# Four edits in the prologue of a Fourier mixing and tanh-shrink kernel: an earlier load, two moves on another queue, a load on two queues, another warm-up

## The chip, the cores and the metric

The kernel runs on one core of a Trainium2 chip. The metric is the device time of one execution in microseconds (us); the runs of one kernel are compared by their median. A core has a matrix engine (TensorE, PE in the profile; its weight loads are PEld), three engines for elementwise work (VectorE or DVE, ScalarE or ACT, GpSimd or POOL) and a sync engine (SP) that only issues transfers. Transfers (DMAs) are issued from the queues of SP, ACT and POOL and are carried out by 16 DMA engines that all queues share. Each engine works through its instructions in program order. Matrix products land in PSUM, which PE writes and DVE and ACT read; everything else on the chip lies in SBUF.

## The reference

The input is 8 batches of 3008 tokens with 256 channels. Per batch, the token axis is Fourier transformed, multiplied with a complex filter and transformed back; then every token goes through a small network with g = h - tanh(h):

```
X = np.fft.rfft(x, axis=1)
Y = X * (filt_r + 1j * filt_i)[None, :, :]
y = np.fft.irfft(Y, n=x.shape[1], axis=1).astype(np.float32)
h = y.reshape(8 * 3008, 256) @ w_in          # 256 x 2048, float64 in
g = h - np.tanh(h)
out = (g @ w_out).astype(np.float32)         # 2048 x 256, float64 in
```

## The kernel before, in words

The length 3008 is split as 64 x 47, so the transform is two steps of small matrix products with a twiddle in between. After the first step the data of one batch is 4 blocks of 32 frequencies by 24 rows. `SLOTS` cuts the 32 frequencies into 7 groups: six of 5 (120 partitions) and a leftover one, group 6, of 2. The leftover group is folded: its 48 rows hold the left half of the channels and 48 more partitions the right half, so it works on 96 partitions with 128 columns. Two transfers inside SBUF do that folding, one for its data and one for its filter; both are the function `under` (L943).

The program has a prologue, for batch 0, and then a long pipeline over groups of tokens (`groups`, 4 units of work each, counted by `U`). From the second token group on, PE has next to no pause; later batches' transforms are worked in between the token products. `first`, `middle` and `last` are generators of that pipeline; `last(0)` (`pu`, L447, copied by ACT to `ut`, L450) begins it, and `up_plain` (L555) follows.

The prologue, in program order:

- Three DMAs' worth of half matrices (`fh`) and x of batch 0 in three chunks `c` of 8 rows (`xs`), each chunk in two halves; the right part of a half comes by POOL's queue. VectorE makes the matrices `f0` from `fh` (L1018, L1021). `filt` is three buffers for filters; the first column block of `filt[2]` is set to 1 and serves as operand of the warm-up.
- `tiled()` (L903): matmuls on these ones whose results nobody reads.
- `first0(c)` (L888): first step for batch 0, 32 PE instructions a chunk (a matmul here is two instructions); the copies (L891) go to ACT, two of the last chunk's to VectorE, into `turnt`.
- Loads of weights. `converted` turns float64 weights into float32 sums by bit work: one load of 512 KB (`raw`, L151), one ACT instruction (L157), six of VectorE (L159 to L177). `jobs[0:5]` are worked in the prologue, the others later; `convert(n)` makes n steps of it.
- `across(g)` (L933, L937): PE transposes group g of `turnt` into a tile `a2`; `forth` (L301): products `pa`, `pb`; `filtered` (L306 to L330): seven to nine instructions, mainly VectorE's, with one of POOL (L327) for groups 0 to 4; `back0` (L970, L972) and, for group 6, `back` (L349): products `pe`, copied by ACT (L975, L352) and written to DRAM as `ct2` (POOL's queue for groups 0 to 4, ACT's for 5, ACT's and SP's for 6).
- The loop over g from 0 to 6 runs these staggered: filters and `across` for g+2, `forth` for g+1, `filtered` for g, `back0` for g-1. `filters_of(g)` (L950, L953) issues six loads (nine for group 6) on POOL for groups 0 and 1 and on SP for the others. A buffer is used again after three groups, so the loads for group g wait for `filtered(g-3)`.
- At g = 3, behind the filters of group 5, SP also issues the matrix `gt` of the first token group (L427, 256 KB) and x of batch 1's first 8 rows (`load_x`, L231, L234, L237, 1 MB in a buffer that an x chunk of batch 0 held).
- After the loop `rest` (L960) reads `ct2` of batch 0 back, turned, as `e2` for the first token group: once for the 25 frequencies of groups 0 to 4, and after `way_back()` of the leftover group for the last 7. Each call is four loads, for four blocks, on SP.
- Behind it, in program order: the first loads of batch 2 (`first`), `convert(100)`, the next weight conversion, `first1` (x of batch 1's first rows through the first step, L1059, L1063, L1064), four steps of weight conversion, and `warmer(10)` (L898), 20 PE instructions whose result nobody reads. Then `pu`.

`under` in the kernel before:

```
def under(t):
    nc.sync.dma_start(t[KL:KH, :, 0:DM // 2], t[0:KL, :, DM // 2:DM])
```

It is called in `across(6)`, which is reached at g = 4, and for the filter at g = 5, ahead of `convert(3)` and `way_back()`.

Of the kernel before, what the change touches and what calls it, by code (L numbers as in the profile page):

```python
# [17 lines left out]
BATCH, SEQ, DM = 8, 3008, 256  # L18
NQ, NR = 64, 47
NA = NQ // 2  # L20
NH = (NR + 1) // 2
SG = 5
# [7 lines left out]
KM = SG * NH  # L30
KL = SLOTS[-1][1] * NH
KH = 2 * KL
# [65 lines left out]
def kernel(  # L98
# [9 lines left out]
    nc = tc.nc  # L108
    V, G, ACT = nc.vector, nc.gpsimd, nc.scalar
# [13 lines left out]
    def dram(t, off, dims):  # L123
        return bass.AP(tensor=t, offset=off, ap=[list(d) for d in dims])
# [86 lines left out]
    def begun(tiles, job, queue=nc.sync):  # L211
        j = converted(tiles, *job, queue)
        next(j)
        return j
# [14 lines left out]
    def load_x(t, b, r, n):  # L229

        nc.sync.dma_start(t[0:64, 0:n, :], dram(x.tensor, (b * SEQ + r) * DM,  # L231
                                                [[NR * DM, 64], [1, n * DM]]))
        if r == 0:
            nc.sync.dma_start(t[64:128, 0, :], dram(x.tensor, b * SEQ * DM,  # L234
                                                    [[NR * DM, 64], [1, DM]]))
        lo = 1 if r == 0 else 0
        nc.sync.dma_start(t[64:128, lo:n, :], dram(x.tensor, (b * SEQ + NR - r - lo) * DM,  # L237
                                                   [[NR * DM, 64], [-DM, n - lo], [1, DM]]))
        return t
# [182 lines left out]
    def load_e2(b, c, parts=None, tiles=None):  # L422

        e2, gt = tiles or (tr.tile([128, CH, DM], F32, tag="e2", bufs=2, name="e2"),
                           tr.tile([128, CH, 128], F32, tag="gt", bufs=2, name="gt"))
        if tiles is None:
            nc.sync.dma_start(gt, g_d[:, CH * 128 * c:CH * 128 * (c + 1)])  # L427
        if parts is None:
            nc.sync.dma_start(e2, dram(ct2[b], CH * c * DM, [[NH * DM, 128], [1, CH * DM]]))
        return e2, gt  # L430
# [422 lines left out]
    with tc.tile_pool(name="tr", bufs=2) as tr, tc.manual_schedule():  # L853
# [12 lines left out]
        with tc.tile_pool(name="pro", bufs=1) as pro, \  # L866
                tc.tile_pool(name="ps0", bufs=6, space=bass.MemoryType.PSUM) as ps0:

            def z0(name, shape):
                return ps0.tile(shape, F32, tag="z", bufs=6, name=name)  # L870
# [3 lines left out]
            def big(shape, dtype, name):  # L874

                return pro.tile(shape, dtype, tag="big", bufs=3, name=name)
# [23 lines left out]
            def tiled():  # L900

                t = filt[2][:, 0]
                banks = [z0("warm", [128, 256]) for _ in range(4)]  # L903

                def mm(rows, cols, bank):
                    nc.tensor.matmul(bank[cols], t[rows, 0:cols.stop - cols.start],
                                     t[rows], start=True, stop=True)

                half = slice(0, 64), slice(64, KM)
                out = slice(0, 64), slice(64, 128)  # L910
                for _ in range(6):
                    mm(slice(0, KM), slice(0, 128), banks[0])
                for n in range(4):
                    for i, rows in enumerate(half):
                        for cols in out:
                            mm(rows, cols, banks[2 * (n % 2) + i])
                for n in range(4):
                    for i, rows in enumerate(half):
                        mm(rows, slice(0, 128), banks[2 * (n % 2) + i])
                for _ in range(2):  # L920
                    mm(slice(0, KM), slice(0, 128), banks[0])

            def across(g):

                a, s = SLOTS[g]
                n = s * NH
                t = tr.tile([KM, 4, DM], F32, tag="a2", bufs=2, name="a2")
                for v in (1, 0):
                    pq = z0("pq", [128, 2, DM])
                    for k in range(2):  # L930
                        at = (2 * v + k) * NA + a
                        for h in range(2):
                            nc.tensor.transpose(  # L933
                                pq[0:n, k, h * 128:h * 128 + 128],
                                turnt[:, h, at:at + s].rearrange("p a r -> p (a r)"), one)
                    copy = ACT.copy if g or v else V.tensor_copy
                    copy(t[0:n, 2 * v:2 * v + 2], pq[0:n])  # L937
                if g == len(SLOTS) - 1:
                    under(t)
                return t  # L940

            def under(t):
                nc.sync.dma_start(t[KL:KH, :, 0:DM // 2], t[0:KL, :, DM // 2:DM])  # L943

            def filters_of(g):

                t, queue = filt[g % 3], G if g < 2 else nc.sync
                if g == len(SLOTS) - 1:
                    V.memset(t[0:1, 2:4], 0.0)
                    queue.dma_start(t[NH:KL, 2:4], dram(filt_d, (turned * 4 + 2) * DM,  # L950
                                                        [[4 * DM, NH], [1, 2 * DM]]))
                for v, row, n, src in filter_rows(g):
                    queue.dma_start(t[row:row + n, v], src)  # L953
                return t

            def rest(a, n, queues):

                e2 = e2s[0][0]
                for j in range(4):
                    queues[j % len(queues)].dma_start(  # L960
                        e2[NA * j + a:NA * j + a + n],
                        dram(ct2[0], (NA * j + a) * NH * DM, [[NH * DM, n], [1, CH * DM]]))
# [39 lines left out]
            for c in range(3):  # L1002
# [16 lines left out]
                for to, cols in ((64, slice(0, 64)), (95, slice(63, 64)), (127, slice(31, 32))):  # L1019
                    n = cols.stop - cols.start  # L1020
# [26 lines left out]
            def convert(n):  # L1047

                for _ in range(n):
                    next(early, None)  # L1050
# [3 lines left out]
            def first1(x1):  # L1054

                for r in range(0, 8, 2):
                    pf = z0("pf", [128, 2, DM])
                    for k in range(2):
                        nc.tensor.matmul(pf[:, k], f0[:, r + k], x1[:, r + k],  # L1059
                                         start=True, stop=True)  # L1060
                    a1 = (pro.tile([128, 2, DM], F32, tag="e1", bufs=5, name="a1") if r < 4 else
                          tr.tile([128, 2, DM], F32, tag="a1", bufs=2, name="a1"))
                    ACT.copy(a1, pf)  # L1063
                    (ACT if r < 4 else nc.sync).dma_start(  # L1064
                        dram(ct1[1], r * DM, [[NH * DM, 128], [1, 2 * DM]]), a1)
                    yield
# [3 lines left out]
            last_g = len(SLOTS) - 1  # L1070
            summed = (last_g,)

            def there0(g):
                there = forth(g, a2.pop(g), z0)
                xy = next(there)
                next(there)
                return there, xy
# [3 lines left out]
            def way_back():  # L1081

                product, what = ended.pop(0)
                for _ in product(*what) or ():
                    pass
# [4 lines left out]
            for g in range(last_g + 1):  # L1090
                if g + 2 <= last_g:
                    fts[g + 2] = filters_of(g + 2)
                    a2[g + 2] = across(g + 2)
                if g == 3:
                    e2s[0] = load_e2(0, 0, ())
                    ones_1 = first1(load_x(big([128, 8, DM], F32, "x1"), 1, 0, 8))
                if g == last_g - 1:
                    under(fts[last_g])
                    convert(3)
                    way_back()  # L1100
                if g < last_g:
                    there[g + 1] = there0(g + 1)
                next(there[g][0])
                if g < last_g - 1:
                    convert(3)
                xy = there.pop(g)[1]
                chain = filtered(g, xy, fts.pop(g), V, V if g >= last_g - 1 else G, pro)
                nn = next(chain)
                for _ in range(2):
                    next(chain)  # L1110
                if g in summed:
                    next(chain)
                ended.append((back, (0, g, xy, z0, (ACT, nc.sync))) if g in summed else (back0, (g, nn)))
                if g not in (0, last_g - 1):
                    way_back()
                if g == 2:
                    ahead = [begun(tiles1, job, queue=G) for job in jobs[5:7]]
            rest(0, SG * (last_g - 1), [nc.sync])
            way_back()
            rest(SG * (last_g - 1), NA - SG * (last_g - 1), [nc.sync])  # L1120
            fs = first(2, z1, [(1, c) for c in range(4, NX)])
            next(fs)
            convert(100)
# [9 lines left out]
        with tc.tile_pool(name="dn", bufs=2) as dn, \  # L1133
# [59 lines left out]
            for U in range(total + 2):  # L1193
                i, u = divmod(U, 4)
# [120 lines left out]
```

## Time and profile before

| what | value |
|---|---|
| runs shown | 2701.81, 2702.39, 2700.45 us; median 2701.81 |
| profiled execution | 2702.15 us, span of its instructions 2700.3 us |
| TensorE clock granted, mean | 0.998 |
| warm-up (L906) | 64 PE instructions, 1.45 to 11.13 us |
| `first0` (L888) | 96 PE instructions, 11.13 to 22.0 us |
| VectorE, 40 to 60 us | 15.9 of 20 us busy |
| first product of the token work (`pu`, L447) | 85.44 us |
| PE idle from 0 to 120 us | 15.8 us |
| PE idle from 160 us to the end | 12.4 of 2540 us |
| moved in the first 110 us | 25.32 MB, mean 230 GB/s |

How to read it: times are from the start of the span. A line of the timeline has the start, the length, engine, line, operation, out<-in, the shape (for PE, rows*columns of the array, then the moving operand), the count, and in brackets the idle time ahead of it and what ended it. An engine with a q is its queue: it waits or issues a transfer. In the list of waits the numbers are the total in us, how often, and the longest. The chain of waits goes back from the last instruction, at each step to what released it. A DMA line in it runs from issue to landing. The granted clock is 1.00 at full speed.

### The profile page before, as it was taken

What the parts mean: (1) busy time and instruction counts of PE and PEld (TensorE: products, weight loads), DVE (VectorE), ACT (ScalarE), POOL (GpSimd) and SP (SyncE); (2) the same over time, 40 slices, a digit from 0 to 9 for tenths busy, and PEclk for the clock granted to TensorE, in tenths of its full rate; (3) what the DMA queues carried; (4) which work ended last, traced back from release to release, by engine and by line L of the source; (5) the groups of instructions that cost most, each with busy time, mean ns of one, the idle gap of its engine ahead of it and who ended that gap; (6) DMA issues with size and microseconds to landing.
All of it is one profiled execution on the core that took longest, in us unless ns stands there. A gap on an engine that the chain in (4) does not pass through costs nothing.

```text
span 2700.3 us, 36549 instructions
## 1 busy us (share of the span) xinstructions
PE 2670.9 (99%) x12950; PEld 2360.7 (87%) x12950; DVE 1651.3 (61%) x2083; ACT 1722.8 (64%) x2595; POOL 1289.9 (48%) x1082
## 2 busy tenths in 40 slices
PE   8999999999999999999999999999999999999998
PEld 7578889988898888988889888898889988898887
DVE  6777766666566664666546665566655666544545
ACT  3566666666666666666666666666666666666665
POOL 4124555454454445545445554455445554554552
PEclk9999999999999999999999999999999999999999
DMA  8754223431242223323233232323322231110110
GB/s 219 233 162 115 56 58 77 107 86 49 63 110 75 80 56 78 98 69 81 54 96 80 68 86 57 92 76 79 88 55 58 52 79 34 31 40 19 24 24 18
DMA packets 341400, 208.09 MB, mean 77 GB/s; under 512 B 227096, under 2 KB 303492, under 8 KB 341144
## 3 DMA queue, kind: packets, MB, share of 16 engines
q1 hardware_dynamic: 298957, 147.45, 22.6%
q10 hardware_dynamic: 38138, 45.63, 5.5%
q0 software_dynamic: 4112, 12.60, 1.7%
q8 instruction: 104, 1.70, 0.3%
q14 instruction: 89, 0.72, 0.1%
HBM read 133.42 MB, written 74.97 MB: 77 GB/s over the span
## 4 chain that ended last, share of the span: by engine, by line
PE 93%; DMA 2%; DVE 2%; ACT 1%; issue 1%; SPq 1%; ACTq 0%; POOL 0%; DVEq 0%
PE o L655 40%; PE x L485 23%; PE z L485 11%; PE y L485 6%; PE pu L447 3%; PE pe L349 3%; PE pf L262 2%; PE pa L301 2%; PE pb L301 1%; PE o L709 1%; DMA gt<-g 0%; DMA mats_sb<-mats 0%; DMA f<-f 0%; ACT y L597 0%; PE o L555 0%
## 5 line engine op out<-in xcount | busy, mean ns | idle before, releaser
L655 PE MATMUL o<-t,wd 128*128 128x256 f32 (+1 forms) x3008 | 759.7, 375 | 0.0
L607 DVE TENSOR_TENSOR h<-h,y 128x1024 f32<-128x1024 f32 (+1 forms) x384 | 513.3, 1337 | 295.7 <-ACT y L603 295.2
L465 POOL TENSOR_TENSOR t<-h 128x512 f32<-128x512 f32 (+1 forms) x186 | 254.1, 1366 | 907.7 <-DVE h L607 836.1
L655 PEld LDWEIGHTS o<-t,wd 128*128 128x128 f32 x3008 | 570.5, 190 | 67.2
L485 PE MATMUL x<-tu,wu 128*128 128x256 f32 (+1 forms) x2256 | 573.0, 376 | 1.6 <-ACT u L491 1.1
L655 PE MATMUL o<-h,wd 128*128 128x256 f32 (+1 forms) x2256 | 570.4, 375 | 1.8 <-DVE h L607 1.8
L485 PEld LDWEIGHTS x<-tu,wu 128*128 128x128 f32 x2256 | 421.5, 190 | 57.5 <-ACT u L491 9.6
L655 PEld LDWEIGHTS o<-h,wd 128*128 128x128 f32 x2256 | 424.2, 190 | 50.3 <-DVE h L607 2.6
L491 ACT COPY s<-x 128x512 f32<-128x512 f32 (+1 forms) x188 | 108.6, 578 | 501.9 <-PE x L485 483.8
L597 ACT ACTIVATE y<-h 128x1024 f32<-128x1024 f32 (+1 forms) x384 | 400.2, 1042 | 13.3 <-ACT a L263 5.2
L600 ACT ACTIVATE y<-y 128x1024 f32<-128x1024 f32 (+1 forms) x384 | 399.2, 1039 | 12.1
L603 ACT ACTIVATE y<-y 128x1024 f32<-128x1024 f32 (+1 forms) x384 | 399.9, 1041 | 7.8 <-DMA x_sb<-in_x_dram 2.7
L525 DVE TENSOR_TENSOR h<-z,u 128x512 f32<-128x512 f32 (+1 forms) x188 | 127.5, 678 | 243.8 <-ACT u L491 243.1
L468 POOL TENSOR_TENSOR t<-h,t 128x512 f32<-128x512 f32 (+1 forms) x186 | 264.3, 1421 | 0.0
L491 ACT COPY u<-x 128x512 f32<-128x512 f32 (+1 forms) x376 | 214.5, 571 | 76.9 <-PE x L485 50.5
L467 POOL TENSOR_TENSOR t<-h 128x512 f32<-128x512 f32 (+1 forms) x186 | 262.9, 1413 | 0.0
L466 POOL TENSOR_TENSOR t<-h,t 128x512 f32<-128x512 f32 (+1 forms) x186 | 255.9, 1376 | 14.6
L533 DVE COPY h<-x 128x512 f32<-128x512 f32 (+1 forms) x188 | 127.9, 680 | 152.8 <-PE x L485 152.2
L485 PE MATMUL x<-ut,wu 128*128 128x256 f32 (+1 forms) x752 | 190.2, 375 | 0.0
L485 PE MATMUL y<-ut,wu 128*128 128x256 f32 (+1 forms) x752 | 190.1, 375 | 0.0
L485 PE MATMUL z<-ut,wu 128*128 128x256 f32 (+1 forms) x752 | 190.1, 375 | 0.0
L485 PE MATMUL z<-tu,wu 128*128 128x256 f32 (+1 forms) x752 | 190.0, 375 | 0.0
(153 smaller groups left out, 3037.4 us busy)
## 6 DMA issues: line engine op xcount, KB each, us to landing
e<-ct SPq DMA_DIRECT2D x47, 512.0 KB
ct<-a ACTq DMA_DIRECT2D x82, 256.0 KB
ct<-e ACTq DMA_DIRECT2D x86, 240.0 KB
a<-ct SPq DMA_DIRECT2D x42, 480.0 KB
ft<-filt SPq DMA_DIRECT2D x42, 480.0 KB
out_dram<-ot SPq DMA_DIRECT2D x1248, 16.0 KB
x_sb<-in_x_dram SPq DMA_DIRECT2D x154, 128.0 KB
gt<-g SPq DMA_DIRECT2D x48, 256.0 KB
```

The lines of the kernel that those rows point to most:

```text
L465: by.tensor_sub(t[0], b[0][1], b[0][0])
L466: by.tensor_sub(t[1], b[1][1], t[0])
L467: by.tensor_sub(t[2], b[1][1], b[0][1])
L468: by.tensor_sub(t[3], b[1][0], t[1])
L485: nc.tensor.matmul(bank[:, k], wu[:, q - 1, (2 * u + k) * 128:(2 * u + k + 1) * 128], rhs[q - 1], start=(first and k == 0), stop=True, ski ...
L491: ACT.copy(t, X)
L533: V.tensor_copy(h[:, 2, :, 0:w], X)
L597: ACT.activation(y[k], ht[k], AF.Arctan, scale=TURN)
L600: ACT.activation(y[k], y[k], AF.Tanh, scale=BEND)
L603: ACT.activation(y[k], y[k], AF.Square, scale=SCALE, accum_out=y_sums[:, 2 * U + k // 2:2 * U + k // 2 + 1])
L607: V.tensor_mul(ht[k], ht[k], y[k])
L655: nc.tensor.matmul(product(q), wd[:, q - 1, (2 * u + k) * 128: (2 * u + k + 1) * 128], rhs[q - 1][:, k], start=(u == 0 and k == 0 and q == ...
```

## The change

Four edits, all in the prologue:

1. Warm-up: `tiled()` gets other matmuls. Before: 6 whole-array matmuls of 256 columns, 16 on quarters of the array, 8 on halves, 2 whole. After: 6 whole ones of 256 columns, 3 whole ones of 64 columns; 2 whole, 4 on quarters; 2 whole, 8 on quarters; 2 whole, 8 on halves of 64 columns; 2 whole, 16 on tiles of 24 rows by 24 columns; 1 whole. Each matmul is two PE instructions: 64 before, 108 after.
2. `under` issues on POOL's queue (`G`) instead of SP's.
3. `gt` of the first token group and x of batch 1 are issued at g = 1 instead of g = 3.
4. The second `rest`, for the last 7 frequencies, uses SP's and ACT's queues in turn.

```diff
-                def mm(rows, cols, bank):
-                    nc.tensor.matmul(bank[cols], t[rows, 0:cols.stop - cols.start],
-                                     t[rows], start=True, stop=True)
+                def mm(rows, cols, bank, n=256):
+                    nc.tensor.matmul(bank[cols, 0:n], t[rows, 0:cols.stop - cols.start],
+                                     t[rows, 0:n], start=True, stop=True)
 
                 half = slice(0, 64), slice(64, KM)
-                out = slice(0, 64), slice(64, 128)
-                for _ in range(6):
-                    mm(slice(0, KM), slice(0, 128), banks[0])
-                for n in range(4):
+                full, out = slice(0, 128), (slice(0, 64), slice(64, 128))
+
+                def whole(k, n):
+                    for i in range(k):
+                        mm(slice(0, KM), full, banks[i % 2], n)
+
+                whole(6, 256)
+                whole(3, 64)
+                for k in (1, 2):
+                    whole(2, 256)
+                    for _ in range(k):
+                        for i, rows in enumerate(half):
+                            for cols in out:
+                                mm(rows, cols, banks[2 + i])
+                whole(2, 256)
+                for _ in range(4):
                     for i, rows in enumerate(half):
-                        for cols in out:
-                            mm(rows, cols, banks[2 * (n % 2) + i])
-                for n in range(4):
-                    for i, rows in enumerate(half):
-                        mm(rows, slice(0, 128), banks[2 * (n % 2) + i])
-                for _ in range(2):
-                    mm(slice(0, KM), slice(0, 128), banks[0])
+                        mm(rows, full, banks[2 + i], 64)
+                whole(2, 256)
+                for i in range(4):
+                    for j in range(4):
+                        rows, cols = (slice(32 * k, 32 * k + 24) for k in (i, j))
+                        mm(rows, cols, banks[i])
+                whole(1, 256)
...
             def under(t):
-                nc.sync.dma_start(t[KL:KH, :, 0:DM // 2], t[0:KL, :, DM // 2:DM])
+                G.dma_start(t[KL:KH, :, 0:DM // 2], t[0:KL, :, DM // 2:DM])
...
-                if g == 3:
+                if g == 1:
                     e2s[0] = load_e2(0, 0, ())
                     ones_1 = first1(load_x(big([128, 8, DM], F32, "x1"), 1, 0, 8))
...
-            rest(SG * (last_g - 1), NA - SG * (last_g - 1), [nc.sync])
+            rest(SG * (last_g - 1), NA - SG * (last_g - 1), [nc.sync, ACT])
```

## The prediction

> **What bounds the kernel now.** First the page, then busy times by stage.
>
> ```profile
> PE 2670.9 (99%) x12950; PEld 2360.7 (87%) x12950; DVE 1651.3 (61%) x2083; ACT 1722.8 (64%) x2595; POOL 1289.9 (48%) x1082
> ```
> ```profile
> 0.00:120.00 120.00, 104.21 (x522) 78.32 (x523) 82.38 (x146) 55.57 (x93) 38.55 (x58) 0.99 0.85 230
> ...
> 160.00:2700.00 2540.00, 2527.65 (x12283) 2255.95 (x12281) 1534.33 (x1865) 1640.34 (x2460) 1250.59 (x1023) 1.00 0.27 68
> ```
> After the length, the columns are the busy times of PE, weight loads, DVE, ACT and POOL, the granted clock, the DMA share and GB/s. After 160 us PE runs without a hole worth naming (2527.65 of 2540), so whatever moves the start of the token work moves the end by as much. Every edit lies ahead of 85.44 us, where `pu` (L447) starts that work. The question is when `pu` starts and how fast PE runs behind it. Next the timeline of PE:
>
> ```profile
> 1.45 9.85 PE L906 MATMUL warm<-filt 120*128 120x256 f32 x64 [1.45 <-DVE filt L1000]
> 11.13 10.88 PE L888 MATMUL pf<-f,x 128*128 128x128 f32 x96
> 22.95 1.06 PE L933 MATMUL pq<-one_sb,wd 128*120 128x128 f32 x8 [0.94 <-ACT wd L891]
> ```
> ```profile
> 79.41 4.48 PE L898 MATMUL warm<-f 128*128 128x256 f32 x20
> 85.44 1.97 PE L447 MATMUL pu<-gt,e 128*128 128x128 f32 x16 [1.55 <-DMA x_sb<-in_x_dram]
> ```
> The 96 matmuls of `first0` start the moment the warm-up (L906) ends: nothing is idle between. From 24.05 to 46.5 VectorE then works with no gap. So warm-up, `first0`, `across(0)` and VectorE's filters are one chain. The late part is in the chain of waits:
>
> ```profile
> 67.58 4.17 DMA filt<-filt
> ...
> 76.11 5.12 DMA ct<-e
> 81.26 0.04 issue
> 81.30 0.30 SPq L960
> ...
> 85.44 1.97 PE pu L447 x16
> ```
> The reader sees the leftover group's move inside the chip (L943) land at 71.75, its result written at 76.11, and the remaining tokens (L960) issued only at 81.30.
>
> **Part 1, the warm-up.** A matmul here is two instructions. Their single starts: whole-array ones of 256 columns lie 0.427 us apart until the clock rises near 5.8, then 0.216. The first twelve are the same before and after, so the old rest runs from 6.26 to 11.13: 4.87 us. It is 8 sets of four quarter-array instructions, 8 pairs of half-array ones and 4 whole ones, 20 slots of 0.216 = 4.32; the other 0.55 goes to 3 changes of shape, 0.185 each. The new rest: 18 whole instructions (3.89), 24 quarter ones = 6 sets (1.30), 6 whole ones of 64 columns, 16 half ones of 64 columns = 8 pairs, 32 instructions on 32-row tiles, 8 changes of shape (1.48). No row has a warm-up matmul of 64 columns: the `pu` of 64 columns follow each other by 0.059, while the weight loads beside them keep 0.112. Each new one has its own load, so I take 0.112: 0.67 and 0.90, with 0.35 and 0.47 as the low end. Nor is there a 32-row tile: one whole, two halves or four quarters fill one slot, so sixteen should, and 32 instructions are 2 slots (0.43); four at a time, as in the nearest row, it is 8 slots (1.73). Sum 3.89 + 1.30 + 0.67 + 0.90 + 0.43 + 1.48 = 8.67, so `first0` starts near 14.9 and **3.8 us later**. Low 2.4 (short columns at 0.059, 0.1 a change of shape), high 5.1. The data hide none of it: by the semaphore updates the last half of x lands at 17.94, and PE starts that half at 11.13 + 5 x 1.79 = 20.1. There are 2.1 us of slack already, which is also the most that a shorter warm-up could win.
>
> **Part 2, x of batch 1 sooner.** Nothing is added; `gt` (256 KB) and x1 (1 MB) move in SP's queue from behind the filters of group 5 to ahead of those of groups 4 and 5. The four issues took 2.8 us there (47.93 to 50.77). In this trace the DMA share is 0.49 from 40 to 47.5 and 0.97 from 47.5 to 62.5, so the load goes to an emptier place. SP's and ACT's issues take eight completion semaphores in turn, and each waits for the DMA eight before it. So two of group 4's filter issues and two of group 5's now wait for these loads. They landed 9.9 to 15.1 us after issue in the full stretch; I estimate 4 to 8 in the emptier one. Group 4's filters land near 49 (before the shift of part 1) and are read at 57.90; group 5's near 54, read at 64.54. Cover 9 us, price 0; without it each us of lateness would be VectorE's. The gain is that group 6's filters are no longer held: their issues ran from 54.15 to 65.58, and should end near 58.
>
> **Part 3, the leftover group's moves by GpSimd.**
>
> ```profile
> DVE nn L318 <- DMA filt<-filt: 1.2, 1, 1.2
> ```
> ```profile
> PE pa L301 <- DMA a<-a: 0.8, 1, 0.8
> ```
> On POOL each issue costs some 0.75 (its other issues: 0.72 to 0.77). `a<-a` falls behind the two `ct<-e` that end at 57.0 and ahead of L327 at 61.35, where POOL was idle. `filt<-filt` falls behind those that end at 64.3 and lands near 68 (3.5 to 4.2 as its neighbours); behind it stand two `ct<-e`, not ready before 65.7 and 69.2. So `pa` no longer waits and starts at the end of `back0(4)`, 67.9; L306 comes 0.6 sooner, and with the 1.2 of L318 the last group is 1.8 sooner. I book nearly none of it. The result's landing is late for another reason: of the 16 arrivals of the `ct<-e` issued at 76.11 on ACT, eleven came by 78.42 and five at 80.80 to 81.23. The same five-fold tail stands in `e<-ct` (25 rows on five DMA engines), in two 512 KB `raw` loads issued at 70.14 and 70.87, and in group 5's `ct<-e`. Those five engines are never out of work from 70 to 81.5, and none of that load starts sooner. I take -0.2, between 0 and -1.8.
>
> **Part 4, remaining tokens by two queues.** SP's four L960 issues take 81.30 to 82.64; two go to ACT, so the last one lands 0.7 sooner. But ACT's issues wait for `ct<-e` too, and this is what stands behind them in its queue:
>
> ```profile
> 77.41 0.68 ACT L157 ACTIVATE top<-raws 128x512 f32<-128x512 f32 x1 [0.51 <-ACT e L352]
> 77.99 0.57 ACT L1063 COPY a<-pf 128x512 f32<-128x512 f32 x1
> ...
> 81.16 1.07 ACT L1063 COPY a<-pf 128x512 f32<-128x512 f32 x2 [0.42 <-ACT a L1063]
> 82.12 0.69 ACT L157 ACTIVATE conv<-raw 128x512 f32<-128x512 f32 x1
> 86.60 0.53 ACT L450 COPY ut<-pu 128x448 f32<-128x448 f32 x1 [3.79 <-DMA f<-f]
> ```
> Two L157 (1.36), four L1063 (2.3) and their two DMA issues (0.7), 4.4 us in all, now begin at 82.0 and end near 86.4; `ut` comes no sooner than 86.5 against 86.60. Price 0, between -0.7 and +0.7. Behind it, VectorE's conversions wait, and with them POOL's `raw` load of 86.19: 3.5 us later. From 91 to 105 the DMA share is 1.04 and PE stands idle 1.85 for it; a load started late in a full stretch costs something: +0.6, between -1 and +2.
>
> There is a second effect on PE. Its filling work (L1059, L898) follows the last group and now ends 1.8 sooner, near 82.0, while `pu` stays at 85.4: idle for 3.4 us instead of 1.55. What that does is in these stages (length, PE busy, granted clock, DMA share, GB/s):
>
> ```profile
> 57.00:60.40 3.40, 1.88 (x9) 1.00 1.06 192
> 60.40:63.80 3.40, 1.52 (x6) 1.00 0.79 219
> 63.80:67.20 3.40, 3.40 (x10) 0.50 0.61 174
> ...
> 84.30:87.70 3.40, 2.26 (x18) 1.00 0.69 199
> ```
> A stretch of 3.4 us with 1.52 busy was followed by 3.4 us at half clock; 1.88 and 2.26 were not. Idle for 3.4, PE has under 1.7 busy in one such stretch wherever it falls. Half clock on work without a hole costs 1.7; I take 1.4, since part of it may fall into the idle time (0 to 1.7). [...]
>
> **The sum.** 3.8 + 0 - 0.2 + 0 + 0.6 + 1.4 = +5.6. The profiled run took 2702.15 (span 2700.3, 1.85 around it), 0.34 over the runs' median of 2701.81: 2702.15 + 5.6 - 0.34 = **2707.4**.
>
> **Rivals.** (a) No drop of the clock and no DMA price: 3.8 - 0.2 = +3.6, 2705.4. For it: the stretches that set the clock may cut the idle time in two, and the line between 1.52 and 1.88 isn't known. Against: 3.4 us is more than twice the old idle time. (b) Not slower: the last group's 1.8 us go through, because the five engines get group 5's and 6's results earlier and end earlier; with 0.7 of part 4 and the drop at 63.8 gone as PE no longer waits (1.1 us: the eight L970/L972 groups from 62.95 took 4.6 instead of 3.5), -3.6 stands against a warm-up of +2.4 to +3.8: 2700.6 to 2702.0. It decides if `ct<-e` lands within 3.5 us of its issue. For it: a `ct<-e` at 63.58 did so. Against: the five late arrivals. It would need the 1.85 of idle time at 102 as well to pass 0.2%. (c) The warm-up brings no delay, since its tiles run inside each other's slots, and the rest is as in (b): about 2698. Against: starts 0.216 apart even with four tiles at once. (d) ACT's held queue starves weights or x loads in the first token group: a further 3 to 6 us of idle PE, 2710 to 2713. Against: the third unit of token work needs its weights at 104.95, and they would be ready near 90.
>
> **How the numbers follow.** Forecast 0.47, (a) 0.27, (b) 0.13, (c) 0.04, (d) 0.09. The line of 0.2%, about what a measurement of this kernel can tell from no change, is 5.4 us: 2707.2. The forecast's own spread (2705.5 to 2709.5) lies across it: 0.33 of its 0.47 above, with (d) and 0.12 of (a)'s upper bounds 0.54. Faster by 0.2% needs (c) and part of (b): 0.05. The rest, 0.41, is within. Range 2701.6 to 2711.5: it leaves out half of (b), (c) and the end of (d).
>
> **What would show it.** First L888 near 14.9 (right) or under 12 (wrong). L943 on POOL, no wait of L318 for `filt<-filt`. `ct<-e` of group 6 issued near 78 and landing near 85 (82 if (b)). ACT idle for some 6 us ahead of L157. PE idle over 3 us ahead of `pu`, then half clock. The forecast fails if `pu` starts before 87.

## The result, and the profile after

The changed kernel takes 2707.26 us (median of 20 runs, 2705.03 to 2709.27), the kernel before beside it 2702.26 (20 runs, 2699.31 to 2705.14): 1.0018 times as long, interval 1.0011 to 1.0025, or 5.0 us. Single executions of one kernel differ by several us, and the longer ones had the lower granted clock: of the 107 executions of the kernel before that ran beside the experiments, 54 with a mean clock of 0.998 took 2700.87 us on average, 28 with 0.997 took 2702.89, and 21 with 0.996 took 2704.33. The profiled execution of the changed kernel has a span of 2705.0 us. Twelve lines were added in `tiled`, so what stood behind L905 now stands 12 lines lower (L960 is L972, L1063 is L1075).

By stages of the changed kernel (length, busy times of PE, weight loads, DVE, ACT and POOL, granted clock, DMA share, GB/s):

```profile
0.00:120.00 120.00, 104.04 (x550) 79.60 (x551) 76.57 (x135) 49.97 (x84) 39.23 (x59) 0.97 0.78 217
160.00:2700.00 2540.00, 2533.31 (x12301) 2259.19 (x12299) 1537.41 (x1874) 1644.08 (x2465) 1250.59 (x1023) 1.00 0.27 68
```

The long rest is as full as before. In the first 120 us PE was busy for as long as before (104.04 against 104.21), but with 44 more warm-up instructions and at a granted clock of 0.97 instead of 0.99. The timeline of PE shows where:

```profile
1.45 13.56 PE L906 MATMUL warm<-filt 120*128 120x256 f32 x108 [1.45 <-DVE filt L1012]
14.85 10.88 PE L888 MATMUL pf<-f,x 128*128 128x128 f32 x96
...
81.36 4.48 PE L898 MATMUL warm<-f 128*128 128x256 f32 x20
90.97 3.62 PE L447 MATMUL pu<-gt,e 128*128 128x128 f32 x16 [5.14 <-ACT a L1075]
94.43 1.80 PE L555 MATMUL x<-ut,wu 128*128 128x448 f32 x4
...
109.19 1.03 PE L262 MATMUL pf<-x_sb,f 128*128 128x256 f32 x4
110.05 1.67 PE L555 MATMUL x<-ut,wu 128*128 128x448 f32 x4
```

The lines of the kernel before to compare with, as far as they stand nowhere above:

```profile
87.25 1.80 PE L555 MATMUL x<-ut,wu 128*128 128x448 f32 x4
...
104.02 1.10 PE L262 MATMUL pf<-x_sb,f 128*128 128x256 f32 x4 [1.85 <-DMA f<-f]
104.95 1.67 PE L555 MATMUL x<-ut,wu 128*128 128x448 f32 x4
```

`first0` starts 3.72 us later, `pu` 5.53 later after 5.14 us of idle time, and takes 3.62 instead of 1.97; `x`, the first L555, starts 7.18 later (94.43 against 87.25). What `pu` waits for stands on ACT:

```profile
78.83 0.37 ACTq L354 DMA_DIRECT2D ct<-e  x1
86.35 0.72 ACTq L972 DMA_DIRECT2D e<-ct  x2
87.18 0.66 ACT L157 ACTIVATE top<-raws 128x512 f32<-128x512 f32 x1 [8.38 <-DMA e<-ct]
...
89.84 1.07 ACT L1075 COPY a<-pf 128x512 f32<-128x512 f32 x2 [0.44 <-ACT a L1075]
90.80 0.68 ACT L157 ACTIVATE conv<-raw 128x512 f32<-128x512 f32 x1
93.14 0.53 ACT L450 COPY ut<-pu 128x448 f32<-128x448 f32 x1 [1.66 <-DVE conv L165]
```

From 79.2 to 86.35 ACT's queue holds at its first L972, until group 6's results have landed. The chain of waits has the same step, 8.27 us for a transfer that took 5.12 before:

```profile
78.06 8.27 DMA ct<-e
...
86.81 3.14 DMA e<-ct
...
90.33 0.60 ACT a L1075
90.93 0.04 issue
90.97 3.62 PE pu L447 x16
```

Between the last remaining-token load (landed at 90.12) and `pu` (90.97) now stands a copy of ACT, which ends at 90.91. In the kernel before the last load landed at 85.06 and `pu` followed at 85.44. The stages around `pu` (columns as above):

```profile
87.60:91.00 3.40, 0.03 (x1) 0.03 (x1) 2.96 (x6) 2.45 (x6) 0.00 (x0) 1.00 0.81 243
91.00:94.40 3.40, 3.40 (x16) 3.40 (x17) 3.11 (x7) 1.01 (x2) 0.00 (x0) 0.50 0.98 303
94.40:97.80 3.40, 3.40 (x11) 1.72 (x11) 2.57 (x5) 1.66 (x4) 0.71 (x1) 1.00 0.95 307
```

All of `pu` runs at half clock. Of the 7.18 us at `x` only 5.1 are left at the third unit of token work (110.05 against 104.95): the 1.85 us for which PE stood idle ahead of 104.02 in the kernel before are gone. And of the folding, the list of VectorE's waits from 60 to 80 us has one line left:

```profile
DVE xy L306 <- ACT xy L304: 0.7, 1, 0.7
```

L318 of the leftover group no longer waits for the filter; it comes 1.95 us later than before behind a `first0` that is 3.72 later, so 1.8 us were won there.

### The profile page after: what moved, and what is told of

It is laid out like the page before. It is cut to its first block, busy times and chain, and to the rows that moved or that the text cites. A ratio compares the mean times of both kernels' runs of the same rounds, so it can differ in the third digit from the quotient of the medians.

```text
span 2705.0 us, 36638 instructions
## 1 busy us (share of the span) xinstructions
PE 2676.5 (99%) x12994; PEld 2364.7 (87%) x12994; DVE 1650.8 (61%) x2083; ACT 1722.4 (64%) x2595; POOL 1291.2 (48%) x1084
## 4 chain that ended last, share of the span: by engine, by line
PE 94%; DVE 2%; ACT 2%; DMA 1%; issue 1%; SPq 0%; ACTq 0%; POOL 0%; DVEq 0%; POOLq 0%
PE o L655 39%; PE x L485 23%; PE z L485 11%; PE y L485 6%; PE pu L447 3%; PE pe L349 3%; PE pf L262 2%; PE pb L301 2%; PE pa L301 1%; PE o L709 1%; PE warm L906 1%; PE o L555 0%; DMA ct<-e 0%; PE pf L888 0%; ACT y L597 0%
```

## The experiments

Landings are read from the semaphore updates of the transfers: the last of the four `ct<-e` (L354) of group 6. "Last raw" is the issue of the second of the two 512 KB loads that GpSimd issues around 70 us. A dash: the raws follow later. "Idle" is PE's idle time right ahead of `pu`; "third x" is the start of the third unit of token work, behind the place where the kernel before waits at 104.02. The time is the median, the ratio goes against runs of the kernel before on the same chip, with its 95% interval. All columns from "profiled" on come from one profiled execution each, whose time stands there: e2's was 2.9 us shorter than its median and e3's 3.2 longer, so differences of 1 to 3 us between profiles prove little.

| kernel | time | ratio | profiled | first L888 | last raw | L354 last issue | landed | idle | first L555 | third x |
|---|---|---|---|---|---|---|---|---|---|---|
| before | 2702.26 | | 2702.15 | 11.13 | 70.87 | 76.93 | 81.54 | 1.55 | 87.25 | 104.95 |
| changed | 2707.26 | 1.0018 (1.0011 to 1.0025) | 2706.84 | 14.85 | 74.51 | 79.28 | 86.52 | 5.14 | 94.43 | 110.05 |
| e1 | 2706.33 | 1.0018 (1.0009 to 1.0027) | 2705.56 | 14.42 | 73.94 | 78.63 | 85.01 | 3.41 | 91.41 | 108.02 |
| e2 | 2703.83 | 1.0008 (0.9999 to 1.0017) | 2700.97 | 11.00 | 70.70 | 75.58 | 81.85 | 4.08 | 88.57 | 105.26 |
| e3 | 2703.28 | 1.0006 (0.9997 to 1.0015) | 2706.48 | 10.57 | 72.55 | 76.87 | 83.24 | 3.88 | 91.18 | 109.02 |
| e4 | 2703.64 | 1.0006 (0.9997 to 1.0015) | 2705.06 | 11.77 | 72.19 | 81.70 | 84.75 | 5.13 | 92.08 | 107.82 |
| e5 | 2706.13 | 1.0014 (1.0005 to 1.0023) | 2705.69 | 14.99 | 74.48 | 79.60 | 85.50 | 0.76 | 92.52 | 108.11 |
| e6 | 2709.62 | 1.0025 (1.0016 to 1.0035) | 2709.65 | 15.46 | - | 79.74 | 83.67 | 1.59 | 94.06 | 112.12 |
| e7 | 2704.64 | 1.0008 (0.9999 to 1.0017) | 2704.64 | 15.07 | 74.57 | 83.20 | 84.75 | 3.08 | 92.44 | 109.18 |
| e8 | 2702.25 | 0.9998 (0.9989 to 1.0007) | 2702.52 | 8.52 | 69.82 | 74.54 | 80.94 | 4.19 | 88.73 | 104.99 |
| e9 | 2700.61 | 0.9994 (0.9985 to 1.0003) | 2698.82 | 10.64 | 74.47 | 74.52 | 80.22 | 2.88 | 86.17 | 101.78 |
| e10 | 2701.83 | 1.0002 (0.9993 to 1.0011) | 2703.41 | 8.99 | 74.62 | 75.18 | 82.32 | 3.40 | 88.98 | 105.58 |
| e11 | 2699.93 | 0.9989 (0.9980 to 0.9998) | 2699.46 | 10.84 | - | 75.43 | 78.35 | 1.04 | 85.23 | 102.53 |
| e12 | 2706.80 | 1.0015 (1.0006 to 1.0024) | 2705.74 | 14.48 | 73.97 | 78.34 | 85.79 | 4.62 | 93.05 | 108.90 |

**e1, the new warm-up alone; e2, all but the new warm-up.** e1 is the kernel before with the new `tiled`, e2 the changed kernel with the old one.

> The kernel before with the new warm-up alone. Theory W (the warm-up is nearly the whole loss): first0 starts near 14.85, every step of the prologue keeps its distance to it, pu starts near 85.4 + 3.7 = 89.1 after an idle time of about 1.5 us, no half clock behind it; 3.7 us slower than before. Rival Q (the second queue's wait and the half clock are the loss; a later start is won back where PE waits for transfers, 1.85 us at 102): at most 2 us slower, with the wait at pf gone.

> The changed kernel with the old warm-up, so the earlier load, the folding by GpSimd and the two queues. Theory W: 5.0 - 3.7 = 1.3 us slower than before (0 to 2): the folded group 1.8 us sooner, its result on DRAM hardly sooner, pu held by ACT's copies after more than 3 us of idle PE, half clock behind it, some 2 us of that won back at the transfers near 102. Rival Q: 3 us slower or more. Third view (the folding's 1.8 us go through to pu): 1 us faster or more.

e1 takes 4.3 us more than the kernel before (2702.04 in this series), e2 1.8, with an interval that reaches just below nothing. So the warm-up costs 4.3 put in alone and 3.2 taken out (5.0 less 1.8): most of the loss either way, as booked, though the two do not add up to 5.0. e1 also missed a part of what was expected: PE is idle for 3.41 us, not 1.5, and the clock falls.

```profile
89.00 2.62 PE L447 MATMUL pu<-gt,e 128*128 128x128 f32 x16 [3.41 <-DMA x_sb<-in_x_dram]
91.41 2.79 PE L555 MATMUL x<-ut,wu 128*128 128x448 f32 x4
```

So the half clock does not need the folding. e2 answers for the folding: its results leave at 74.24 to 75.58, 1.3 to 1.9 us sooner than before, and land at 81.29 to 81.85, 0.3 later than before. Nothing of what the folding won arrives. No run has the folding or the earlier load by itself.

**e3, the two queues alone; e4, the earlier load and the folding alone.**

```diff
 e3, on the kernel before
-            rest(SG * (last_g - 1), NA - SG * (last_g - 1), [nc.sync])
+            rest(SG * (last_g - 1), NA - SG * (last_g - 1), [nc.sync, ACT])
 e4, on the kernel before
-                nc.sync.dma_start(t[KL:KH, :, 0:DM // 2], t[0:KL, :, DM // 2:DM])
+                G.dma_start(t[KL:KH, :, 0:DM // 2], t[0:KL, :, DM // 2:DM])
-                if g == 3:
+                if g == 1:
```

> The kernel before with the last 7 frequencies loaded by SP and ACT, nothing else. Theory W: ACT idles from 77.4 to 81.3, its copies end near 86, pu starts 0 to 0.7 us later than 85.44 after some 2 us of idle PE, no half clock; within 1 us of before. Rival Q: 2 us slower or more.

> The kernel before with the earlier load and the folding by GpSimd's queue, old warm-up, SP alone for the last 7 frequencies. Five-engine theory: L318 of the folded group starts near 70.3 instead of 72.04, but the five late arrivals of ct<-e stay at 80.5 or later, pu gains under 0.6 us; PE idles 3 us ahead of pu and may fall to half clock (up to 1.7 us). 0 to 1.5 us slower than before. Rival (the gain goes through): ct<-e lands near 79.7, pu near 83.7, 1.7 us faster.

Both medians lie above the one before (+1.2 and +1.6), both intervals hold 1; a gain is not there in either. e3's profile has `pu` at 87.71 with 3.88 us of idle time and half clock, where at most 86.1 and no half clock were expected; but that execution was late already at the raw loads (72.55 against 70.87), which stand ahead of the edit. What part 4 brings is in the order of its trace; first ACT, then PE, from 83 us:

```profile
83.94 0.66 ACT L157 ACTIVATE top<-raws 128x512 f32<-128x512 f32 x1 [7.15 <-DMA e<-ct]
...
90.09 0.53 ACT L450 COPY ut<-pu 128x448 f32<-128x448 f32 x1 [1.86 <-DMA ct<-a]
```
```profile
87.71 3.68 PE L447 MATMUL pu<-gt,e 128*128 128x128 f32 x16 [3.88 <-DMA ct<-a]
91.18 2.81 PE L555 MATMUL x<-ut,wu 128*128 128x448 f32 x4
```

`ut` starts 0.17 us after the second store of `first1` (`ct<-a`) has landed at 89.92. So it is in every kernel here with part 4: 93.04 and 93.14 in the changed kernel, 87.89 and 87.98 in e2, 91.84 and 91.94 in e5, 93.38 and 93.48 in e6, 91.42 and 91.75 in e7. In the kernel before that store had landed at 82.80 and `ut` came at 86.60. ACT's held queue delays not only the copies but also their stores, and `ut` waits for those. The source has the reason: `ut` lies in the pool `dn`, which opens where the prologue's pool `pro` closes, and the two tiles that ACT stores lie in `pro`; `pu` lies in a PSUM pool that opens where `first1`'s closes, so it waits for `first1`'s copies. From the last load's landing to `pu` it takes 0.81 to 1.23 us in the six profiles with part 4, and 0.34 to 0.70 in the eight without. The late `ut` itself holds up PE in two of them alone, for 0.52 us in e5 and 4.11 in e6; elsewhere `pu` itself lasts until then. e4 shows another wait: the fourth L354 issue, on SP, went out at 81.70, since the load eight issues before it landed at 81.63.

**e5, longer filling.** On the changed kernel:

```diff
-            warmer(10)
+            warmer(18)
```

> The changed kernel with 18 instead of 10 matmul pairs in the filling work ahead of pu (L898): 3.6 us more of it, so PE is idle for some 1.5 us ahead of pu instead of 5.1. Clock theory (the drop to half clock behind pu costs the time it showed, 1.65 us): no stretch of half clock behind pu, the first L555 follows pu by about 1.9 us instead of 3.5, and the time falls by 1 to 1.7 us, to some +3.5 over the kernel before (2705.7). Rival (what PE gains there it waits for at the transfers of the first token group, since in the kernel before PE stood 1.85 us for them): the first L555 comes 1.6 us sooner, a wait of about that size appears before 112 us, and the time stays within 0.5 us of the changed kernel's 2707.2.

```profile
90.01 2.00 PE L447 MATMUL pu<-gt,e 128*128 128x128 f32 x16 [0.76 <-ACT a L1075]
92.52 1.77 PE L555 MATMUL x<-ut,wu 128*128 128x448 f32 x4 [0.52 <-ACT ut L450]
```

`pu` runs at full clock, `x` comes 1.9 us sooner than in the changed kernel, and no new wait follows before 120 us. Of the 1.9, 0.95 lie between the start of `pu` and `x` (2.51 instead of 3.46, with 0.52 of waiting for `ut` that the half clock had covered). The other 0.96 is an earlier `pu`: group 6's results landed at 85.50 instead of 86.52, though the two programs are the same up to there, so this part is scatter. The time is 1.1 us less, inside what the clock theory gave; the intervals of the two kernels overlap, so the trace carries this more than the medians. That the idle time brings the half clock is shown (0.76 us of it here, 5.14 in the changed kernel); what it costs is about 1 us here.

**e6, the raw loads later; e7, the 25-row loads cut.** Ahead of the last five arrivals the DMA share of the changed kernel is 0.30 to 0.35 (83.2 to 84.7 us), about that of five engines of 16 at work. Two theories name what these had to move first: the two raw loads, and the first remaining-token loads of 25 rows each. On the changed kernel:

```diff
 e6
+            G.tensor_copy(gate96, e2s[0][0][96:97, 0, 0:1])
             late = weights(tiles1, jobs[5:], G, ahead, 3,
 e7
-            rest(0, SG * (last_g - 1), [nc.sync])
+            rest(0, 16, [nc.sync])
+            rest(16, SG * (last_g - 1) - 16, [nc.sync])
```

> The changed kernel with the two raw loads that GpSimd issues at 73.79 and 74.51 held back until the last of the first four remaining-token loads (25 rows each) has landed, by a one-element copy of GpSimd from it. Theory R (the raw loads, 512 KB each, are what holds the five late engines): the ct<-e of group 6 land within 4.6 us of their issue instead of 7.7, pu starts 2 to 3 us sooner, and the time is 2704 to 2705.5. Theory F (the 25-row loads themselves, 400 KB on five engines, are what holds them): the five late arrivals stay, the landing comes at most 1.5 us sooner, and the time stays within 1 us of 2707.2, or rises where the raws are now late for their conversion.

> The changed kernel with each of the first four remaining-token loads of 25 rows cut in two, of 16 and of 9 rows (eight issues of SP instead of four, same bytes). Theory F (25 rows are spread on five DMA engines, and these five bring the last arrivals of everything issued behind): the 16 rows come as 16 arrivals, the five-fold tail of the ct<-e of group 6 goes, they land 4 to 5.5 us after issue instead of 7.7, pu starts 2 to 3 us sooner, and the time is 2704 to 2705.5. Theory R (the raw loads hold them): the tail stays within 1 us of where it was, and the time within 1 us of 2707.2.

Updates per transfer, and the L354 of ACT issued last:

```
          25 rows   16 rows   9 rows   7 rows   L354 issued: first eleven arrivals by, last five from, to
changed      6                            8     78.83: 83.13, 85.12, 86.52
e6           6                            8     79.37: 81.05, 82.52, 83.47
e7                    16        10        8     78.88: 82.54, 82.74, 83.31
```

Each theory holds half. Without the raws ahead (e6) the tail of five stays, but ends 3.9 us after the last issue instead of 7.2. Without the 25-row loads (e7) the arrivals come evenly, and this L354 lands 4.4 us after its issue. In these runs the raws make all arrivals late (the first eleven came within 4.30 us of the issue, in e6 within 1.68), and the 25-row loads make the last five later still (within 7.69, in e7 within 4.43). In e7 SP's two L354 issues went out only at 82.75 and 83.20: its four extra loads moved the turn of the completion semaphores, and the first of them waited for the one of the `ct<-e` that landed at 82.69. Still e7's median is 2.6 us under the changed kernel's (2703.18 to 2706.37 against 2705.03 to 2709.27); its profile shows 0.9 of it at the third unit (109.18 against 110.05), the rest comes later and is not explained. e6's is 2.4 above it, in spite of its `pu`:

```profile
87.96 2.00 PE L447 MATMUL pu<-gt,e 128*128 128x128 f32 x16 [1.59 <-ACT a L1076]
94.06 3.35 PE L555 MATMUL x<-ut,wu 128*128 128x448 f32 x4 [4.11 <-ACT ut L450]
```

`pu` comes 3.0 us sooner. But the raws, issued at 83.81 and 84.53, now move beside the loads and stores behind the last `rest` (90 to 95 us: DMA share 1.05); the store for which `ut` waits lands at 93.38, and the idle time moves from ahead of `pu` to behind it, half clock included. `x` starts no later than in the changed kernel, but it and the product behind it run at half clock (92.25 to 99.08), and the third unit is 2.1 us later (112.12 against 110.05).

**e8, a shorter warm-up.** On the kernel before, 10 slots less:

```diff
-                for n in range(4):
+                for n in range(2):
                     for i, rows in enumerate(half):
                         for cols in out:
...
-                for n in range(4):
+                for n in range(1):
                     for i, rows in enumerate(half):
```

> The kernel before with a shorter warm-up: 4 sets of quarter-array and 2 pairs of half-array matmuls instead of 8 and 8, 10 slots of 0.216 us less. Theory W (the warm-up lies on the one chain that sets the end, so its length passes through both ways until the data of x are the limit): the first L888 starts near 9.0 instead of 11.13, the half of x that comes last (17.94) is then just in time, and the time falls by 1.5 to 2.1 us, to some 2700.4. Rival T (what comes sooner is swallowed by the transfers behind, as the 1.8 us of the folded group were in the run without the new warm-up): group 6's ct<-e are issued 2.1 us sooner but land at 81.2 to 81.5 as before, and the time falls by less than 0.7.

The time does not move: rival T. `first0` starts 2.6 us sooner and meets the data of x (0.21 us of idle time at 12.47); VectorE's chain is 1.6 to 1.9 sooner, group 6's results leave 2.4 sooner and land 0.6 sooner. PE is then idle for 4.19 us and runs `pu` at half clock, so `x` comes 1.5 later than before; the wait at 104.02 is missing, and the third unit starts where it did (104.99 against 104.95). So in these two runs the warm-up passes through in one direction: longer, it moves raws, 25-row loads and results (e1: 3.1, 3.1 to 3.5 and 1.7 us later, landing 3.5 later); shorter, the results run into the same transfers.

**e9, e10, e11, towards a faster kernel.** On e4; e10 is e9 with e8's warm-up; e11 is e9 with the raws behind the 9-row loads:

```diff
 e9
-            rest(0, SG * (last_g - 1), [nc.sync])
+            rest(0, 16, [nc.sync])
+            rest(16, SG * (last_g - 1) - 16, [G])
 e11, on e9
+            G.tensor_copy(gate96, e2s[0][0][96:121, 0, 0:1])
             late = weights(tiles1, jobs[5:], G, ahead, 3,
```

> The kernel before with the earlier load and the folding by GpSimd (parts 2 and 3), and with each of the first four remaining-token loads cut in two: 16 rows by SP, 9 rows by GpSimd, behind its last ct<-e and ahead of the two raw loads, which so go out 3 us later. The last rest stays on SP alone, the warm-up is the old one. Theory F+R (the 25-row loads on five engines and the two raw loads ahead of them hold the landing of group 6): group 6's ct<-e, issued at 74.2 to 75.6 as in the run without the new warm-up, land by 80 instead of 81.3 to 81.9, pu starts at 82.5 to 84, right behind the filling work, with no half clock, and the time is 2699.5 to 2701.5. Rival D (transfers behind pu set the end of this stage, as the 1.85 us of idle time near 102 in the kernel before): pu starts as early, but PE stands idle for the difference before 112 us and the time is within 1 us of 2702.2.

> The kernel of the run before it in this list, with the shorter warm-up as well (4 and 2 sets instead of 8 and 8, first L888 near 8.5). Theory F+R: with the landing freed, the 2.6 us that the shorter warm-up wins pass through: group 6's ct<-e issued near 72 and landed by 77.5, pu at 80 to 81.5, time 2697.5 to 2700. Rival D: idle time before 112 us takes it back, time 2701 to 2702.5.

> The kernel e9 (earlier load, folding by GpSimd, first remaining-token loads of 16 rows by SP and 9 by GpSimd) with GpSimd's two raw loads also held until the last 9-row load has landed, by a copy of GpSimd from those rows: the raws go out near 76.2 and 77 instead of 73.72 and 74.47. Theory F+R: all four ct<-e of group 6 land within 4 us of issue (by 78.5; in e9 the second pair took 5.1 and 5.7), pu follows the filling work by less than 1.5 us, no half clock, and the time is 2698 to 2700. Rival D (transfers behind pu set the end): the raws' conversions or the loads of the first token group are late by as much, and the time is that of e9 or more, 2700.5 to 2703.

e9 lands sooner (80.22), keeps the clock, and its median is 1.5 us below that before; the interval holds 1. Its raws went out at 73.72 and 74.47, 3.6 us later than before, as expected; `pu` came at 84.36, a little outside the 82.5 to 84 expected, after 2.88 us of idle time. e10 wins nothing more. In the one profile its chain had lost the shorter warm-up's lead by 49.6 us (VectorE's L159 at 49.55, as in e9), and with 3.40 us idle it fell to half clock; which of the two is the rule was not tried. e11 does what the theory says up to `pu`: the results land 2.9 us after their last issue, `pu` follows the filling work by 1.04. Its raws went out at 78.54 and 79.27, 2.3 later than expected. It is faster than the changed kernel (its slowest run took 2700.87, that kernel's fastest 2705.03), and by its interval (0.9980 to 0.9998) narrowly faster than the kernel before. In its series the kernel before ran at 2703.74, in the others at 2702.0 to 2702.3, so of the 3.8 us between the medians some 1.5 may be that series; with a mean clock of 0.998 e11's eight executions took 2699.87 on average, against 2700.87 for the 54 of the kernel before, so much of its gain is that the clock falls less often. Against e9 it wins little, for the timeline of PE shows the wait of the kernel before again:

```profile
101.59 1.10 PE L262 MATMUL pf<-x_sb,f 128*128 128x256 f32 x4 [1.20 <-DMA x_sb<-in_x_dram]
...
104.79 1.10 PE L262 MATMUL pf<-x_sb,f 128*128 128x256 f32 x4 [0.60 <-DMA x_sb<-in_x_dram]
```

From 85 to 105 us its DMA share is 1.03 to 1.07. So the wait that rival D speaks of is there in e11, though the time is in the other theory's range. It does not follow from an early `x` alone: e9's `x` is earlier than the kernel before's as well, and e9 has no such wait.

**e12, the changed kernel with its last loads on SP alone.**

```diff
-            rest(SG * (last_g - 1), NA - SG * (last_g - 1), [nc.sync, ACT])
+            rest(SG * (last_g - 1), NA - SG * (last_g - 1), [nc.sync])
```

> The changed kernel with its last remaining-token loads on SP alone again (part 4 undone, parts 1 to 3 kept). Theory A (two queues let ACT's held queue set the start: pu and ut wait for ACT's copies and their stores): pu no longer waits for ACT, ut follows pu's first half at once, the first L555 comes 0.3 to 1.5 us sooner, and the time is 2705.7 to 2707. Rival S (what ACT holds lies in the shade of pu's half clock and of the loads, and part 4 costs nothing within the changed kernel): SP's issues land 0.7 later, pu starts with them, and the time is 2707 to 2708.

`pu` starts at 89.92, 0.49 us after the last of the loads landed at 89.43, `ut` follows its first half, and `x` comes 1.4 sooner than in the changed kernel. The median is 0.5 below the changed kernel's; against the kernel before in its own series (2703.74, as for e11) it is +3.1 instead of +5.0. The intervals overlap, so these runs do not tell the gain from nothing. In the trace it is theory A; in the time both remain possible.

## Why the prediction was right

The forecast was 2707.4; measured were 2707.26 and, against the runs beside it, +5.0 where the sum had said +5.6. The mechanism held in its two large terms, the warm-up and the half clock. That the time was met within 0.2 us is luck: at `pu` the delay was 5.53 where the terms up to there gave 3.6, and behind `x` 2.1 us fell away where 0.6 had been added, so the errors nearly cancelled; besides, the base of 2701.81 was 0.45 under the 20 runs beside the changed kernel. Slower by more than 0.2% had been given 0.54; measured is 0.18%, with an interval on both sides of that line.

**Warm-up, +3.8: right.** `first0` starts 3.72 later in the profile; over the six profiles with each warm-up it starts at 14.88 and 10.99 on average, 3.9 apart. In time it is +4.3 alone (e1), 3.2 taken out (e2). The single starts give the parts: 64-column instructions 0.105 to 0.112 us apart, as taken; the 32 instructions on 32-row tiles go sixteen at once, two slots, as taken. The "2.1 us of slack" named as the most that a shorter warm-up could win was not passed: in e8 PE meets the data, and VectorE's chain gains 1.6 to 1.9.

**Earlier load, 0: not contradicted.** `gt` and x1, issued at 39.6 to 41.4, landed 2.9 to 6.5 us later, and group 6's filters were issued by 61.4 and there by 64.5. No run has this edit alone.

**Folding, -0.2: right that no gain arrives, too low in this profile.** The 1.8 us were won at L318, and the five late arrivals were named as the reason to book none (in the kernel before the DMA share was 0.30 to 0.34 from 78.5 to 80.5 us, about that of five engines of 16 at work). But the landing was taken as fixed relative to the warm-up, and it came 4.98 us later where `first0` came 3.72 later: 1.26 more. In e5, the same program up to there, it came 3.96 later where `first0` came 3.86 later: 0.1 more. So the term lies between 0.1 and 1.3 in these two profiles. e2 and e4 place this: folding and earlier load alone do not make anything faster, and e2's landing is that of before. e6 and e7 show the two causes apart, the raws and the 25 rows. From the last raw issue to the landing it was 10.7 us before, 11.1 in e1, 11.2 in e2 and 12.0 here: the landing is nearer to a constant behind the raws than behind its own last issue (4.6 to 7.2). Why 12.0 here and 11.0 in e5 is left open. In the semaphore updates, a transfer on the queues of SP and ACT has 6 updates with 25 rows and 8 with 7 (both in the changed kernel, one of them 0.43 to 0.79 us after the issue and the others 2.1 or more after it), 10 with 9 rows and 16 with 16 (e7).

**Two queues, 0: mis-sized, +0.5 at `pu`.** The 0.7 of issue time was not won: from the results' landing to the last L972 landing it was 3.6 us, 3.5 before. The sum saw ACT's 4.4 us behind the wait and held them against `ut` at 86.5. It missed that `pu` itself waits for the last of those copies (90.91, `pu` at 90.97), and that `ut` waits for their stores. Alone it is +1.2, with an interval that includes no change (e3), and e12 wins 0.5, not told from nothing, by taking it out.

**Half clock, +1.4: right, with half of its reason.** It is 1.65 at `pu` (3.46 against 1.81 from its start to `x`), 0.95 of which e5 wins back there, and 1.1 in time by e5. The reason given was that the filling work ends 1.8 sooner against `pu`; it does (85.84 against 83.89, where `first0` is 3.72 later), but `pu` also came 1.8 later than `first0` explains, by the landing and by ACT, and e1 falls to half clock without the folding.

**Raw load late in a full stretch, +0.6: wrong sign, -2.1.** The stretch of 91 to 105 us was read as one more thing to be late for. The `raw` load was issued at 94.89 instead of 86.19, 8.7 us later and not 3.5, and no cost shows: the wait of 1.85 ahead of the fourth `pf` is gone. Why it is gone is open. It stands in three of the fourteen profiles: before, e3 (0.97, at 108.08) and e11 (1.20 and 0.60). It is missing in the other eleven, and among them is e9, whose `x` starts earlier than the kernel before's (86.17 against 87.25). So a later `x` is not enough to explain it, and the -2.1 may belong to the one profile of the kernel before rather than to the change.

In the profiles: 3.72 + 1.26 (landing) + 0.08 (loads) + 0.47 (ACT) = 5.53 at `pu`, + 1.65 = 7.18 at `x`, - 2.1 by the third unit, and some 0.4 less by the end.

**The rivals.** (a), no drop of the clock, falls with the 3.40 us at 0.50. (b), the gains go through, set its own test: a landing within 3.5 us of the issue; it took 6.7 to 8.3; and the drop of the clock at 63.8 that it took as gone came at 67.109. Its aim can be reached by other edits: e11, with the raws moved and the 25-row loads cut, meets the test (2.7 to 2.9) and is the faster kernel. (c), no delay by the warm-up, falls with e1. (d) had the right place, ACT's held queue, and too high a price: it cost stores and `ut`, and in the changed kernel no idle time in the first token group.

## What to carry to other kernels

In the changed kernel ACT's queue held for a late transfer from 79.2 to 86.35 us, and so held everything behind it, and the stores of that work too; list them, down to the tiles whose memory they free, before moving an issue to a busier engine. When a result is late in landing, look at how its arrivals are spread: the loads of 25 rows had 6 updates each, and cutting them into 16 and 9 rows, with 16 and 10 updates, moved the median by 2.6 us here. And a chain that passes a delay on need not pass a gain on: try it in both directions. Before a wait seen once is booked as a part of a kernel, see whether it stands in other profiles: the one of 1.85 us here stood in three of fourteen.

## What the runs showed of the hardware

Ahead of `pu` (and of `x` in e6), PE was idle for 0.76 (e5), 1.04 (e11), 1.55 (before), 1.59 (e6) and 2.88 us (e9) and kept its clock: `pu` took 1.97 to 2.00. After 3.08 (e7), 3.40 (e10), 3.41 (e1), 3.88 (e3), 4.08 (e2), 4.19 (e8), 4.62 (e12), 5.13 (e4) and 5.14 us (changed) it ran at half clock for all or part of `pu`, which took 2.50 to 3.68, and after 4.11 in e6 for `x`, which took 3.35 where it took 1.80 in the kernel before. But the length of one pause is not what decides in these profiles. In the changed kernel half clock came at 67.11 after pauses of 1.84 and 1.57 us (to 64.57 and to 66.80), both shorter than the 2.88 of e9 that brought none; from 63.70 to 67.11 PE was busy for 0.97 of 3.41 us. In the 3.41 us ahead of the half clock at 91.00 it was busy for 0.03, and ahead of that at 63.79 in the kernel before for 1.50. Each of these three stretches at half clock lasted 3.41 us. What decides is not shown.

The instructions of the warm-up's matmuls of 24 rows and 24 columns start 0.007 us apart in the changed kernel, sixteen in a row, against 0.216 from one that fills the array to the next.
